# One of three int16 shifts of a softmax group moved from VectorE to GpSimd, with a smaller backlog limit and a wider pace limit

## Chip, cores, metric

One core of one Trainium2 chip. The metric is the device time of one execution in microseconds (us). The kernel before took 1766.27 us (median of 3 runs, 1764.87 to 1768.45).

Engines are named as in the profile: PE (matmuls; PEld is its weight load), ACT (ScalarE), DVE (VectorE), POOL (GpSimd), SP (DMA issue). "Granted clock" is the PE clock that the throttle let through, as a share of full speed.

## The reference, cut to what matters

Two layers, each attention and then a gated feed-forward block (2048 tokens, width 512, 32 heads of 16, feed-forward width 1792):

```
x = x + attention(layernorm(x));  x = x + ffn(layernorm(x))      # twice
scores = q @ k.T * 16 ** -0.5;  p = softmax(scores);  o = p @ v  # 32 heads, 2048 x 2048 each
```

The scores make 4096 tiles of 128 x 512 that need an exponential.

## The kernel before

At build time the program runs a time model of all engines and records one fixed instruction order for each ("the plan"). On the chip every engine follows its order and waits on semaphores. A cost in the model that differs from the chip doesn't make the result wrong; it makes the order a bad one.

Exponentials come in groups of 12 tiles, filled in four slots of three tiles. In an ordinary group ACT does all 12. In a *vector group* ACT does two tiles of each slot and DVE the third: it turns the score into the bits of a float16 (tile `fPI`: scale, bias and conversion to int16 give a straight-line approximation of 2^x). To make the approximation better, DVE adds 256, 512 and 768 to the integers (quarter octaves, tiles `fPP`), and PE multiplies all four versions with suitably scaled copies of V. These three additions are the *shifts*, each 128 x 2048 int16.

```python
    DVE_LATE = 3.0          # backlog limit, us of planned DVE work
    LAG = 6                 # pace limit, pieces of the feed-forward stage
    ...
    def port_at(eng, t):    # the plan's model of the shared port: DVE shift against Pool instruction
        for a, b in reversed(port["dve" if eng == "pool" else "pool"][-12:]):
            if a <= t < b:
                return b
        return t
    ...
    def vector_group():
        if pend.get(("PI", dg_no[0] % NPI)):
            return False
        late = max(0.0, sch.free["dve"] - now[0]) + sum(op[3] for j in jobs["dve"] for op in j[2])
        late += 0.6 * len(shifts)
        return late < DVE_LATE
    ...
            # is the next group a vector group?
            d = size == 3 and (layer or u) and vector_group() and behind() < LAG
    ...
            # a_slot: the third tile of a slot, on DVE; after the fourth one, the three shifts
            def then(o):
                ...
                if r == 3:
                    for ph in range(1, NPH):
                        shift(uk, c, g, m, gi, ph)
            dve(0, [(lambda e: e.tensor_scalar(PI[:, gi, 512 * r:512 * (r + 1)], bank(b0 + n - 1), DBIAS, 0.0,
                                               op0=ALU.add, op1=ALU.max), [bks[-1]], [("PI", gi, r)], 0.6)], then)
    ...
    def shift(uk, c, g, m, gi, ph):
        ...
        shifts.append((s, [(lambda e: e.tensor_scalar(PP[:, s, :], PI[:, gi, :], int(OCT) * ph // NPH, None,
                                                      op0=ALU.add),
                            [("PI", gi, r) for r in range(4)], [("PP", s)],
                            2.8 if ph in POOLED else 0.6)], then, ph in POOLED))      # 2.8, 0.6: planned us
    POOLED = ()
    ...
    def behind():           # "post": output projection and feed-forward of a query block, beside the next attention
        ...
        return PIECES * f - pace["n"]
    def post_tol():
        if pace["haste"] or behind() > LAG:
            return 99.0
        return 1.0 if behind() > 0 else 0.1
```

When PE has nothing to do for long, the plan adds filler matmuls (`fONB`,`fZV`) to keep its clock up.

## Time and profile before

| | us |
|---|---|
| span | 1766.0 |
| ACT busy, of it exponentials | 1602.1, 1527.4 |
| PE busy (ends are modelled) | 1614.0 |
| DVE busy, of it conversions / shifts | 1276.4, 504.3 / 393.7 |
| POOL busy | 208.2 |
| vector groups | 192 of 320 (768 conversions / 4) |

From the page of the kernel before: busy us of each engine, the span in 40 slices (tenths busy; PEclk in tenths of full clock), and the chain that ended last.

```profile
PE 1614.0 (91%) x16180; PEld 497.5 (28%) x16349; DVE 1276.4 (72%) x2103; ACT 1602.1 (91%) x1488; POOL 208.2 (12%) x226
...
DVE  5799996577856878538653799767895588856853
ACT  2699889999999999999899999999999999999932
POOL 2502011011110011010330110201011000101000
PEclk9999999999999999999999999999999999999999
...
ACT 61%; PE 21%; DVE 14%; issue 1%; POOL 1%; DMA 1%; SPq 0%; DVEq 0%; POOLq 0%
```

ACT is nearly full (8 or 9 tenths) from the third slice to the third last and makes most of the chain: exponentials are the limit. DVE is full only in the dense stage of slices 3 to 6 and in slices 24, 25 and 30.

Groups of instructions of the kernel before, shapes kept apart. Columns: line, engine, operation, out<-in, shapes, count, then busy us and mean ns of one, then idle time just before and what ended it.

```profile
L1128 ACT ACTIVATE fPT<-fPS 128x1024 bf16<-128x1024 f32 x992 | 932.4, 1078 | 43.2 <-PE fPS L1123 41.5
L1128 ACT ACTIVATE fPT<-fPS 128x1536 bf16<-128x1536 f32 x448 | 611.4, 1509 | 40.0 <-PE fPS L1123 39.5
L1162 DVE TENSOR_SCALAR fPI<-fPS 128x512 int16<-128x512 f32 x768 | 504.3, 683 | 65.5 <-PE fPS L1123 63.9
L1184 DVE TENSOR_SCALAR fPP<-fPI 128x2048 int16<-128x2048 int16 x576 | 393.7, 716 | 4.4 <-PE fPS L1233 3.4
L1253 PE MATMUL fPS<-fONB,fZV 128*17 128x512 bf16 x3356 | 256.6, 386 | 5.0 <-POOL fONB L344 4.1 <-DVE fOS L808 0.8
L651 POOL TENSOR_SCALAR fVD<-fVP 128x544 f16<-128x544 f16 x24 | 38.4, 1600 | 44.8 <-DVE fVP L659 43.4
L545 POOL TENSOR_SCALAR fHT<-fX,fLNS 128x512 bf16<-128x512 f32 x36 | 27.3, 773 | 0.9
L651 POOL TENSOR_SCALAR fVD<-fVP 128x136 f16<-128x136 f16 x24 | 15.5, 648 | 85.7 <-DVE fVP L659 84.4
```

### The profile page before, as it was taken

To read this page: it belongs to the slowest core of one execution; us is meant where nothing else is said; L and a number is where in the kernel's file an instruction comes from. 1 tells how busy PE (TensorE), PEld (TensorE's weight loads), DVE (VectorE), ACT (ScalarE), POOL (GpSimd) and SP (SyncE) were. 2 spreads that over 40 slices of the span, in tenths; PEclk is the share of its full clock that TensorE was granted. 3 is DMA by queue.
4 is the path that set the end of the run, shared out by engine and by line. 5 is a ranking of instruction groups with operands and counts; after the bars stand their busy time and mean duration, and the time that the engine had idled before them with its cause. 6 is when DMAs were issued, how large, how long until landed. Compare 5 with 4: busy or idle time off the path is not lost.

```text
span 1766.0 us, 38383 instructions
## 1 busy us (share of the span) xinstructions
PE 1614.0 (91%) x16180; PEld 497.5 (28%) x16349; DVE 1276.4 (72%) x2103; ACT 1602.1 (91%) x1488; POOL 208.2 (12%) x226
## 2 busy tenths in 40 slices
PE   7898989999899999989999989999989899999998
PEld 3422222222222222332333322222222222222233
DVE  5799996577856878538653799767895588856853
ACT  2699889999999999999899999999999999999932
POOL 2502011011110011010330110201011000101000
PEclk9999999999999999999999999999999999999999
DMA  5200000143111530125214100013401142012513
GB/s 156 73 2 17 2 15 10 47 119 115 41 37 41 162 86 17 43 57 158 65 48 133 41 18 9 17 49 102 148 18 31 51 134 91 23 39 81 152 27 104
DMA packets 138705, 114.00 MB, mean 65 GB/s; under 512 B 12320, under 2 KB 126240, under 8 KB 138528
## 3 DMA queue, kind: packets, MB, share of 16 engines
q1 hardware_dynamic: 134256, 103.07, 20.3%
q0 software_dynamic: 4272, 8.39, 1.7%
q8 instruction: 133, 2.18, 0.5%
q14 instruction: 44, 0.36, 0.1%
HBM read 97.78 MB, written 6.82 MB: 59 GB/s over the span
## 4 chain that ended last, share of the span: by engine, by line
ACT 61%; PE 21%; DVE 14%; issue 1%; POOL 1%; DMA 1%; SPq 0%; DVEq 0%; POOLq 0%
ACT fPT L1128 58%; DVE fPI L1162 6%; PE fPS L575 6%; PE fPS L1123 5%; DVE fPP L1184 5%; PE fPS L1233 4%; PE fPS L1253 3%; ACT fHT L1094 2%; PE fPS L932 2%; DVE fQ L618 1%; PE fPS L638 1%; DVE fHT L545 1%; ACT L1094 1%; DMA fX<-in_A_x_dram 0%; POOL fVD L651 0%
## 5 line engine op out<-in xcount | busy, mean ns | idle before, releaser
L1128 ACT ACTIVATE fPT<-fPS 128x1024 bf16<-128x1024 f32 (+1 forms) x1440 | 1527.4, 1212 | 83.1 <-PE fPS L1123 81.1
L1123 PE MATMUL fPS<-fQ,fKT 32*128 32x512 bf16 x4096 | 554.2, 385 | 71.5 <-ACT fPT L1128 56.0
L1162 DVE TENSOR_SCALAR fPI<-fPS 128x512 int16<-128x512 f32 x768 | 504.3, 683 | 65.5 <-PE fPS L1123 63.9
L1233 PE MATMUL fPS<-fPT,fVP 128*17 128x512 bf16 x3328 | 432.9, 384 | 13.1 <-ACT fPT L1128 6.7
L1184 DVE TENSOR_SCALAR fPP<-fPI 128x2048 int16<-128x2048 int16 x576 | 393.7, 716 | 4.4 <-PE fPS L1233 3.4
L1123 PEld LDWEIGHTS fPS<-fQ,fKT 32*128 32x128 bf16 x4096 | 138.8, 91 | 617.3 <-ACT fPT L1128 527.1
L1233 PE MATMUL fPS<-fPP,fVD 128*17 128x512 f16 x2304 | 302.3, 381 | 6.4 <-DVE fPP L1184 6.1
L1253 PE MATMUL fPS<-fONB,fZV 128*17 128x512 bf16 x3356 | 256.6, 386 | 5.0 <-POOL fONB L344 4.1
L575 PE MATMUL fPS<-fXNT,fWR 128*128 128x512 bf16 x831 | 212.9, 381 | 20.3 <-DVE fHT L918 8.9
L1233 PE MATMUL fPS<-fPI,fVP 128*17 128x512 f16 x768 | 217.4, 384 | 0.5 <-DVE fPP L1184 0.5
L918 DVE TENSOR_TENSOR fHT<-fPS,fHT 128x512 bf16<-128x512 f32 x112 | 77.0, 689 | 140.0 <-PE fPS L575 92.4
L1233 PEld LDWEIGHTS fPS<-fPT,fVP 128*17 128x17 f16 x3328 | 100.0, 87 | 177.4 <-issue 127.2
L767 POOL TENSOR_TENSOR fAT<-fOS,fRB 128x512 bf16<-128x512 f32 x32 | 42.6, 1330 | 830.1 <-DMA fRB<-rscr 784.8
L895 DVE CAST fHT<-fPS 128x512 bf16<-128x512 f32 x98 | 67.5, 689 | 85.4 <-PE fPS L575 85.3
L932 PE MATMUL fPS<-fWR,fHT 128*128 128x512 bf16 x407 | 115.4, 382 | 6.5 <-issue 4.8
L575 PEld LDWEIGHTS fPS<-fXNT,fWR 128*128 128x128 bf16 x896 | 71.9, 97 | 123.2 <-DVE fHT L918 21.6
L1253 PEld LDWEIGHTS fPS<-fONB,fZV 128*17 128x17 f16 x3356 | 77.0, 91 | 84.5 <-issue 40.7
L1233 PEld LDWEIGHTS fPS<-fPP,fVD 128*17 128x17 f16 x2304 | 69.8, 88 | 88.8 <-issue 48.0
L651 POOL TENSOR_SCALAR fVD<-fVP 128x544 f16<-128x544 f16 (+1 forms) x48 | 53.9, 1124 | 130.5 <-DVE fVP L659 127.8
L808 DVE COPY fOS<-fPS 128x512 f32<-128x512 f32 x64 | 43.8, 684 | 23.8 <-PE fPS L1233 23.7
L533 POOL TENSOR_SCALAR fLNS<-fMV 128x4 f32<-128x4 f32 x16 | 6.3, 395 | 460.3 <-DVE fMV L526 460.2
L1233 PEld LDWEIGHTS fPS<-fPI,fVP 128*17 128x17 f16 x768 | 47.4, 88 | 34.2 <-issue 19.3
(60 smaller groups left out, 693.8 us busy)
## 6 DMA issues: line engine op xcount, KB each, us to landing
fWR<-in_B_w_down_dram SPq DMA_DIRECT2D x189, 256.0 KB, 3.0
fWR<-in_B_w_gate_dram SPq DMA_DIRECT2D x56, 256.0 KB, 3.3
fWR<-in_B_w_up_dram SPq DMA_DIRECT2D x56, 256.0 KB, 2.9
fRB<-rscr SPq DMA_DIRECT2D x256, 32.0 KB, 1.8
fX<-in_A_x_dram POOLq DMA_DIRECT2D x7, 1024.0 KB, 5.4
xscr<-fX SPq DMA_DIRECT2D x16, 256.0 KB, 2.1
fX<-xscr SPq DMA_DIRECT2D x4, 1024.0 KB, 6.2
fAT<-fATS SPq DMA_DIRECT2D x128, 16.0 KB, 1.8
```

Source lines behind the costliest of these rows:

```text
L575: ins = e.matmul(bank(bs[0])[:, 0:cols], lhsT=l, rhs=r_, start=(i == 0), stop=(i == n - 1))
L651: job("pool", 2, [(lambda e, dst=dst, src=src, ph=ph: e.tensor_scalar(dst, src, 2.0 ** (-ph / NPH), None, op0=ALU.mult), [("VP", c, k) for ...
L895: evac_job(1, b, [(lambda e: e.tensor_copy(HT[:, ft, :], bank(b)), [BK[b]], [("HT", ft)], 0.6)], got(("gate", layer, qb, ft)))
L918: (lambda e: e.tensor_tensor(HT[:, ft, :], bank(b), HT[:, ft, :], op=ALU.mult), [BK[b], ("HT", ft)], [("HT", ft)], 0.62)], got(("up", laye ...
L932: ins = e.matmul(bank(b)[:, 0:D], lhsT=HT[:, ft, i * 128:(i + 1) * 128], rhs=WR[:, s, jj * D:(jj + 1) * D], start=(ft == 0), stop=(ft == N ...
L1094: sch.op("act", lambda e, lo=lo, hi=hi: e.activation(HT[:, lo:hi, :], HT[:, lo:hi, :], ACTF.Gelu_apprx_tanh), r=keys, w=keys, cost=0.05 + ...
L1123: ins = e.matmul(bank(b0 + k), lhsT=KT[32 * j:32 * j + 32, c, kt * 128:(kt + 1) * 128], rhs=Q[32 * j:32 * j + 32, qs, :], start=True, stop ...
L1128: o = sch.op("act", lambda e: e.activation(PT[:, p, 0:512 * na].rearrange("p (a b) -> p a b", a=na), PS[:, b0:b0 + na, :], ACTF.Exp, scale ...
L1162: dve(0, [(lambda e: e.tensor_scalar(PI[:, gi, 512 * r:512 * (r + 1)], bank(b0 + n - 1), DBIAS, 0.0, op0=ALU.add, op1=ALU.max), [bks[-1]], ...
L1184: shifts.append((s, [(lambda e: e.tensor_scalar(PP[:, s, :], PI[:, gi, :], int(OCT) * ph // NPH, None, op0=ALU.add), [("PI", gi, r) for r ...
L1233: ins = e.matmul(PS[32 * j:32 * j + VW, ACC, :], lhsT=l, rhs=r_, start=a, stop=z, tile_position=(0, 32 * j), skip_group_check=True)
L1253: ins = e.matmul(PS[32 * j:32 * j + VW, ACC, :], lhsT=ZV[:, :], rhs=ones, start=False, stop=False, tile_position=(0, 32 * j), skip_group_c ...
```

## The change

Intent: let Pool, which is 12% busy, take one of the three shifts in groups 0 to 3 of each five, so that DVE can serve more vector groups; admit vector groups only at a smaller DVE backlog; and let the feed-forward pieces fall further behind before vector groups stop.

```diff
-    DVE_LATE = 3.0
+    DVE_LATE = 2.0
...
-    LAG = 6
+    LAG = 24
...
+        pooled = ph == 1 and m < NM - 1
...
-                            [("PI", gi, r) for r in range(4)], [("PP", s)], 2.8 if ph in POOLED else 0.6)], then, ph in POOLED))
+                            [("PI", gi, r) for r in range(4)], [("PP", s)], 2.8 if pooled else 0.6)], then, pooled))
...
-    POOLED = ()
```

## The prediction

> **What bounds the kernel now.** The page's busy table: ScalarE (ACT) 1602 of 1766 us, PE 1614 (ends modelled), VectorE (DVE) 1276, Pool 208. The chain of waits is 61% ACT, nearly all softmax exponentials. Stretches of 44 us show ACT busy 42 us or more in most between 88 and 1678 us; it idles mostly in head and tail. Exponentials leave ACT in "vector groups": of 12 score tiles DVE takes 4. The groups table has 768 DVE conversions: 192 of 320 groups. A vector group turns four 3-tile exponentials (1509 ns, start to start about 1.36 us) into four 2-tile ones (1078 ns, 0.92 us): ACT saves 1.7 us. DVE pays 4 x 0.68 + 3 x 0.68 us, about 4.7; PE pays 3 more quads of matmuls of about 0.22 us.
>
> Where groups are missing: the DVE timeline shows none for about 25 us at the start of each feed-forward ("post") stage (497 to 522 us, 538 to 556 us), because the pieces are more than 6 behind their pace. In dense attention (88 to 221 us) DVE is 93% busy or more.
>
> **What the change does.** (1) One of three shifts of groups 0 to 3 of five goes to Pool: DVE pays 0.68 us less per such group. Estimate for a Pool shift: the Pool normalisation takes 772 ns for 512 columns and small Pool ops about 250 to 330, so about 0.9 ns a column: 2.1 to 2.4 us for 2048. The shift is DVE's four-per-cycle form (2048 elements in 0.6 to 0.68 us); the Trainium skill, "SBUF — State Buffer", section "Who interferes with whom", says that such a DVE instruction and a Pool instruction take a shared port pair exclusively, the second fully blocked. The trace agrees in kind: this shift reaches 1765 ns, the Pool multiply 2298 (median 1271). Per group the port is taken about 2.2 + 1.3 us of 3.7 to 4.2: it fits, tightly. (2) The pace limit 24 admits vector groups in the post's opening and takes urgency from the pieces. (3) The backlog limit 2.0 admits fewer, offsetting part.
>
> **Sum.** Vector groups rise from 192 to about 222: 30 x 1.7 = 51 us less ACT work. PE must do the same pieces in less time, plus 30 x 0.65 = 20 us. Its filler matmuls, 839 quads or about 180 us, leave room on average, almost none in the slices of the down projection (8 to 24 fillers). I take 75%: 38 us. Predicted 1728 us, 1697 to 1757 eight times in ten. Faster by over 2%: 0.52; within 2%: 0.43; slower by over 2%: 0.05.
>
> **What would show it.** Conversions 768 to about 890; exponential busy 1527 to about 1475 us; about 175 shifts on Pool at 2.1 to 2.8 us, Pool busy about 630 us; DVE busy within 5% of 1276; mean DVE shift up from 716 to 800 ns or more by port waits; filler matmuls 3356 down to about 2700; conversions in the openings of the posts; head and tail unchanged within 5 us.
>
> **What would make it wrong.** Port waits longer than the schedule assumed would stall DVE, then ACT through score banks: the gain shrinks or goes. If PE is the limit in post stages, ACT idles there before score matmuls, or posts slip into the layer change or the tail. If the smaller backlog limit rejects as many groups as the rest admits, conversions and time stay. If posts never block vector groups and the port holds, conversions could pass 950 and the time fall below 1697.

## The result

The changed kernel took 2347.45 us (median of 4 runs, 2337.86 to 2438.24), the kernel before 1767.36 us. The ratio is 1.3264 (95% interval 1.3211 to 1.3317). Ratios here and below are the mean time of one kernel's fast runs over the mean of the other's fast runs of the same rounds, so not quite the ratio of the medians. Three of the four runs are fast runs, 2337.86 to 2350.98 us at a granted clock of 0.854 to 0.862, mean 2344.3 us. The profiled run is slow (2438.24 us, clock 0.691), so I take counts and waits from its trace and compare times with fast runs only.

The page of the changed kernel, the same lines:

```profile
PE 2018.8 (83%) x16097; PEld 529.5 (22%) x16097; DVE 1819.6 (75%) x2143; ACT 1618.5 (66%) x1488; POOL 1214.5 (50%) x403
...
DVE  5778888876886877777843878887888778878752
ACT  2676767667766676666678776665776677666641
POOL 2776663454753447535540456535675345544520
PEclk7766666666666676666677766666767667666677
...
PE 49%; DVE 26%; POOL 17%; issue 4%; ACT 2%; DMA 1%; SPq 0%; POOLq 0%; DVEq 0%
```

ACT is no longer full anywhere and has all but left the chain (61% to 2%). DVE and POOL now make 43% of it. The groups of the changed kernel:

```profile
L1128 ACT ACTIVATE fPT<-fPS 128x1024 bf16<-128x1024 f32 x1116 | 1091.3, 1026 | 442.0 <-PE fPS L1123 437.7
L1185 POOL TENSOR_SCALAR fPP<-fPI 128x2048 int16<-128x2048 int16 x177 | 990.6, 5606 | 821.9 <-DVE fPI L1162 781.0 <-PE fPS L1232 35.5 <-DVE fPP L1185 2.6
L1185 DVE TENSOR_SCALAR fPP<-fPI 128x2048 int16<-128x2048 int16 x492 | 813.3, 1690 | 26.2 <-PE fPS L1232 24.9
L1162 DVE TENSOR_SCALAR fPI<-fPS 128x512 int16<-128x512 f32 x892 | 597.2, 685 | 225.7 <-PE fPS L1123 221.0
L1128 ACT ACTIVATE fPT<-fPS 128x1536 bf16<-128x1536 f32 x324 | 458.2, 1451 | 277.1 <-PE fPS L1123 274.9
L1252 PE MATMUL fPS<-fONB,fZV 128*17 128x512 bf16 x2732 | 270.4, 482 | 5.0 <-POOL fONB L344 4.2 <-DVE fOS L808 0.8
```

The counts are those that the prediction named: 892 conversions (about 890), 177 Pool shifts (about 175), 2732 fillers (about 2700). The durations are not. A Pool shift takes 5606 ns; the plan had 2800. A DVE shift takes 1690 ns in the mean. The minimum, median and maximum of each in the changed kernel:

```profile
L1185 DVE TENSOR_SCALAR fPP<-fPI x492: 621/693/5859, 93.5 to 2345.7; 128x2048 int16<-128x2048 int16 x164
L1185 POOL TENSOR_SCALAR fPP<-fPI x177: 5358/5611/6937, 93.5 to 2328.5; 128x2048 int16<-128x2048 int16 x177
```

The DVE shift's median is what it was (683 before, 693 now). Its mean rises because some take as long as a whole Pool shift (5859). The Trainium skill, "SBUF — State Buffer", section "Who interferes with whom", says that a DVE instruction in a mode that uses two ports and a Pool instruction take one shared port pair exclusively, for the whole instruction, so that the second one blocks. I take the shift, 2048 columns in 0.68 us, to be in such a mode. The trace looks like that, but two other things happen at once: PE also waits for the late Pool results, and the PE clock is down. The longest waits of PE's matmuls in the changed kernel (us, times, longest); in the kernel before, they waited 10.6 us for shifts:

```profile
PE fPS L1232 <- DVE fPP L1185: 171.0, 69, 4.9
PE fPS L1232 <- POOL fPP L1185: 143.3, 99, 3.1
```

The experiments take these apart as far as they can.

### The profile page after: what moved, and what is told of

It is laid out like the page before. It is cut to its first block, busy times and chain, and to the rows that moved or that the text cites. A ratio compares the mean times of both kernels' runs of the same rounds, so it can differ in the third digit from the quotient of the medians.

```text
span 2436.4 us, 38363 instructions
## 1 busy us (share of the span) xinstructions
PE 2018.8 (83%) x16097; PEld 529.5 (22%) x16097; DVE 1819.6 (75%) x2143; ACT 1618.5 (66%) x1488; POOL 1214.5 (50%) x403
## 4 chain that ended last, share of the span: by engine, by line
PE 49%; DVE 26%; POOL 17%; issue 4%; ACT 2%; DMA 1%; SPq 0%; POOLq 0%; DVEq 0%
DVE fPP L1185 16%; POOL fPP L1185 15%; PE fPS L1232 14%; PE fPS L575 13%; PE fPS L1123 11%; DVE fPI L1162 5%; PE fPS L1252 5%; PE fPS L932 4%; ACT fPT L1128 2%; PE fPS L638 1%; DVE fQ L618 1%; PE fPS L552 1%; DVE fHT L895 1%; POOL fVD L651 1%; DVE fOKL L734 1%
## 5 line engine op out<-in xcount | busy, mean ns | idle before, releaser
L1185 POOL TENSOR_SCALAR fPP<-fPI 128x2048 int16<-128x2048 int16 x177 | 990.6, 5606 | 821.9 <-DVE fPI L1162 781.0
L1185 DVE TENSOR_SCALAR fPP<-fPI 128x2048 int16<-128x2048 int16 x492 | 813.3, 1690 | 26.2 <-PE fPS L1232 24.9
L1162 DVE TENSOR_SCALAR fPI<-fPS 128x512 int16<-128x512 f32 x892 | 597.2, 685 | 225.7 <-PE fPS L1123 221.0
L1123 PE MATMUL fPS<-fQ,fKT 32*128 32x512 bf16 x4096 | 633.3, 448 | 42.6 <-DVE fPI L1162 19.4
L1232 PE MATMUL fPS<-fPT,fVP 128*17 128x512 bf16 x3204 | 519.3, 454 | 116.3 <-DVE fPP L1185 71.3
L1232 PE MATMUL fPS<-fPP,fVD 128*17 128x512 f16 x2676 | 394.4, 486 | 162.8 <-POOL fPP L1185 96.5
L1232 PE MATMUL fPS<-fPI,fVP 128*17 128x512 f16 x892 | 293.4, 455 | 39.8 <-DVE fPP L1185 34.5
L575 PE MATMUL fPS<-fXNT,fWR 128*128 128x512 bf16 x896 | 300.4, 480 | 27.4 <-DVE fHT L895 19.1
L932 PE MATMUL fPS<-fWR,fHT 128*128 128x512 bf16 x448 | 158.0, 474 | 0.1
L767 POOL TENSOR_TENSOR fATS<-fOS,fRB 128x512 bf16<-128x512 f32 x32 | 49.3, 1540 | 29.4 <-DMA fRB<-rscr 29.4
```

The lines of the kernel that those rows point to most:

```text
L575: ins = e.matmul(bank(bs[0])[:, 0:cols], lhsT=l, rhs=r_, start=(i == 0), stop=(i == n - 1))
L767: job("pool", 1, [(lambda e: e.tensor_tensor(dst, OS[:, os_, :], RB[:, slot, :], op=ALU.mult), [("OS", os_)] + [("RB", slot, j) for j in r ...
L932: ins = e.matmul(bank(b)[:, 0:D], lhsT=HT[:, ft, i * 128:(i + 1) * 128], rhs=WR[:, s, jj * D:(jj + 1) * D], start=(ft == 0), stop=(ft == N ...
L1123: ins = e.matmul(bank(b0 + k), lhsT=KT[32 * j:32 * j + 32, c, kt * 128:(kt + 1) * 128], rhs=Q[32 * j:32 * j + 32, qs, :], start=True, stop ...
L1232: ins = e.matmul(PS[32 * j:32 * j + VW, ACC, :], lhsT=l, rhs=r_, start=a, stop=z, tile_position=(0, 32 * j), skip_group_check=True)
```

## Experiments

Theory: the Pool shift is twice as long as planned, and what costs time is DVE standing behind it at the port. Rivals: PE waiting for late Pool results; the two limits; the PE clock falling by itself; a plan that is merely wrong about a cost.

### e1_no_pool: the limits without the Pool shift

```diff
-        pooled = ph == 1 and m < NM - 1
+        pooled = False
```

> The changed kernel with all three shifts on DVE again; pace limit 24 and backlog limit 2.0 stay. Theory (the Pool shift alone is to blame): 1715 to 1745 us, mean clock at or above 0.98, DVE shifts back to a mean of 700 to 730 ns, conversions 850 or more. Rival (the new limits crowd PE, or the PE clock falls by itself with more vector groups): 1800 us or more with a clock under 0.95.

Measured: 1729.53 us (1728.79 to 1733.58), ratio to before 0.9789 (0.9772 to 0.9805), clock 0.997, 880 conversions. Page line and DVE shifts of this kernel:

```profile
PE 1591.2 (92%) x15951; PEld 492.4 (29%) x16125; DVE 1392.4 (81%) x2299; ACT 1557.6 (90%) x1488; POOL 209.4 (12%) x226
...
L1185 DVE TENSOR_SCALAR fPP<-fPI 128x2048 int16<-128x2048 int16 x660 | 447.2, 716 | 6.0 <-PE fPS L1232 4.2
```

So the limits alone make the kernel 2.1% faster (the interval lies across the 2% mark, but far from 1), and 220 vector groups do not pull the clock down. The whole loss, about 615 us (2344.3 - 1729.5; the kernel before ran at 1767.4 and 1767.9 us beside them), belongs to the Pool shift.

### e2_pool_only: the Pool shift without the limits

```diff
-    DVE_LATE = 2.0
+    DVE_LATE = 3.0
...
-    LAG = 24
+    LAG = 6
```

> The kernel before with only the Pool shift (pace limit 6, backlog limit 3.0). Theory (Pool alone): 2150 us or more, Pool shifts 5.4 to 5.7 us each, DVE shifts with a mean above 1500 ns. Rival (the limits, or their combination with Pool): under 1900 us.

Measured: 2258.63 us, ratio 1.2779 (1.2758 to 1.2801), clock 0.881 to 0.887; 160 Pool shifts with a mean of 5574 ns; 428 DVE shifts with a mean of 1535 ns. It also failed the correctness check by a hair (relative error 0.020005); this version is only a probe of time. The Pool shift does it without the limits.

### e4_probe: the Pool shift by itself

Seven forms of Pool instruction, three of each back to back, appended at the end of the kernel before, where DVE runs no shifts. Five of the forms:

```python
e.tensor_scalar(PP[:, 0, :], PI[:, 0, :], 256, None, op0=ALU.add)                    # the shift: 2048 int16
e.tensor_scalar(PP[:, 0, 0:1024], PI[:, 0, 0:1024], 256, None, op0=ALU.add)          # half of it
e.tensor_scalar(PP[:, 0, 0:1024].bitcast(F32), OS[:, 0, :], 1.0, None, op0=ALU.add)  # 512 float32
e.tensor_scalar(PP[:, 0, 0:512].bitcast(BF), OS[:, 0, :], 1.0, None, op0=ALU.add)    # 512 float32 to bf16
e.tensor_tensor(PP[:, 0, :].bitcast(I32), PI[:, 0, :].bitcast(I32), <int32 constant>, op=ALU.add)   # 1024 int32
```

> The kernel before with seven forms of Pool instruction, three of each, appended in the tail, where DVE runs no shifts. It measures the Pool shift by itself. If Pool is slow by itself (theory): the 2048-element int16 form takes 5.2 to 5.6 us, the 1024-element form about half. If the 5.6 us of the changed kernel are made of waiting for DVE (rival): 2.1 to 2.8 us here. Forms on 32-bit words (1024 int32 elements, two inputs) about 2.5 us. The time of the kernel itself stays within 5 us of the tail's slack plus these ops, about 1810 us.

Measured (one look): 1787.89 us, most of the additions fit the tail. The timeline of Pool in this kernel; columns are start us, us of all three, instruction, count:

```profile
1722.92 16.39 POOL L1420 TENSOR_SCALAR fPP<-fPI 128x2048 int16<-128x2048 int16 x3
1739.40 8.52 POOL L1422 TENSOR_SCALAR fPP<-fPI 128x1024 int16<-128x1024 int16 x3
1748.00 4.63 POOL L1424 TENSOR_SCALAR fPP<-fOS 128x512 f32<-128x512 f32 x3
1752.71 4.64 POOL L1426 TENSOR_SCALAR fPP<-fOS 128x512 bf16<-128x512 f32 x3
...
1762.15 5.83 POOL L1430 TENSOR_TENSOR fPP<-fPI,fCI 128x1024 int32<-128x1024 int32 x3
```

The shift takes 5.46 us (16.39 / 3), though DVE runs no shifts here. DVE is not quite absent: four of its normalisations come up during the first Pool instructions, and the first three take 5.6 us each and end 0.28 us after the Pool shift that they stand behind. So they wait for Pool, not Pool for them; and in e10_probe2 a one-operation shift with no DVE instruction beside it takes 5.44 us (from 1746.29). The Pool shift is slow by itself, not slowed by DVE. From 512 to 2048 columns the time grows by (5.46 - 1.54) / 1536 = 2.55 ns a column, whatever the data type. And the float32 to bf16 form takes 1.55 us for 512 columns, where the normalisation, with the same shapes and types, takes 0.77. Something other than type and size is at work (see the second probe). I timed by blocks of three because the Trainium skill, "Perfetto Trace Analysis", section "GPSIMD Engine Instruction", advises start-to-start spacing for Pool; here single durations (5358 ns at least) agree with it.

### e5_shadow: Pool instructions that nobody waits for

The plan of e1_no_pool, with PE, ACT and DVE unchanged to the instruction, plus one Pool instruction of the same length per group whose output nobody reads.

```diff
+        if ph == 1 and m < NM - 1:
+            was = sch.free["pool"]
+            sch.op("pool", lambda e: e.tensor_scalar(SHD[:, 0:1984], <1984 int16 of WO>, 1, None, op0=ALU.add),
+                   r=[("PI", gi, 3), ("WO",)], w=[("SHD",)], cost=0.0)
+            sch.last_r[("PI", gi, 3)].pop("pool")     # it does not really read PI: nobody waits for it
+            sch.free["pool"] = was                    # and the plan does not see it
```

> The schedule of e1_no_pool instruction for instruction on PE, ACT and DVE, plus a Pool instruction of the same length per group (1984 int16 inputs, reading a weight tile, its output read by nobody), released by the group's last conversion. Nobody waits for its result, so only the shared port can hurt. Theory A (port lock makes DVE's shifts wait): 2000 us or more, DVE shifts with a mean above 1500 ns and maxima near 5.6 us, clock under 0.95. Rival B (PE waits for the late Pool result; the port matters little): within 2% of e1_no_pool.

Measured: 2560.90 us, ratio 1.4482 (1.4458 to 1.4506), clock 0.81. An instruction that produces nothing costs 831 us. One case from the timelines of DVE and Pool in this kernel:

```profile
157.17 1.28 DVE L1163 TENSOR_SCALAR fPI<-fPS 128x512 int16<-128x512 f32 x2
158.37 4.50 DVE L1193 TENSOR_SCALAR fPP<-fPI 128x2048 int16<-128x2048 int16 x1
```

```profile
156.61 5.71 POOL L1188 TENSOR_SCALAR fSHD<-fWO 128x1984 uint8<-128x1984 int16 x1 [6.98 <-DVE fPI L1163]
```

The Pool instruction runs from 156.61 to 162.32. The conversions at 157.17 read PSUM and run through at full speed. The shift that begins at 158.37 takes 4.50 us and ends 0.55 us after Pool. That is the usual case: of the 171 DVE shifts that start while a shadow runs, 168 end only after it. All that time DVE, which works in order, cannot do the next conversion, and a score bank (the PSUM buffer of a score tile) stays occupied. PE feels the late shifts even more directly:

```profile
PE fPS L1240 <- DVE fPP L1193: 508.9, 180, 5.6
```

PE's matmuls with V waited 508.9 us for DVE shifts (13.2 in e1_no_pool), its score matmuls 28.1 us for conversions (5.3), and ACT waited 861.2 us for scores (85.3). So waiting for the results of Pool shifts is not needed for a loss of this size; the port is enough. One rival remains: a shadow also holds up Pool's own useful work behind it. The trace makes it small: the direct waits of other engines for Pool's results come to 32 us in all here and 16 us in e1_no_pool. The trace of this run agrees with the cited section.

### e6_shadow_half and e14_shadow_short: shorter shadows

e6_shadow_half cuts the shadow to 992 columns. e14_shadow_short has all 1984 columns in a faster form (`1, 1.0, op0=ALU.add, op1=ALU.mult`), which the second probe below suggested.

> e5_shadow with the unread Pool instruction cut to 992 columns: about 2.7 us in place of 5.4, the length that the plan of the changed kernel had assumed. e1_no_pool took 1729.5 us, e5_shadow 2560.9. Theory (time that DVE's shifts stand behind Pool instructions, growing faster than their length): 1820 to 2000 us, DVE shifts with a mean of 900 to 1200 ns. Rival (a fixed cost per Pool instruction, whatever its length): over 2300 us.

> The plan of e1_no_pool for PE, ACT and DVE, plus an unread Pool instruction of about 1.9 us per group (two-operation form). If the remaining 56 us of e7_int32 over e1_no_pool are port waits: 1760 to 1800 us, mean DVE shift 780 to 860 ns. If they come from the plan with pooled shifts or from waits for Pool's results: within 1% of e1_no_pool, 1725 to 1747 us.

Measured: e6_shadow_half 1820.25 us (ratio 1.0299), e14_shadow_short 1882.09 us (ratio 1.0655). DVE shifts and shadow of e6_shadow_half, then of e14_shadow_short:

```profile
L1193 DVE TENSOR_SCALAR fPP<-fPI 128x2048 int16<-128x2048 int16 x660 | 546.5, 865 | 4.1 <-PE fPS L1240 2.6
L1188 POOL TENSOR_SCALAR fSHD<-fWO 128x992 uint8<-128x992 int16 x169 | 519.6, 3074 | 738.6 <-DVE fPI L1163 738.5
```

```profile
L1193 DVE TENSOR_SCALAR fPP<-fPI 128x2048 int16<-128x2048 int16 x660 | 594.9, 938 | 3.7 <-PE fPS L1240 2.1
...
L1188 POOL TENSOR_SCALAR fSHD<-fWO 128x1984 uint8<-128x1984 int16 x169 | 349.5, 2068 | 942.4 <-DVE fPI L1163 942.1
```

The four kernels with one and the same plan for PE, ACT and DVE line up by how long DVE's shifts wait, not by how long the Pool instruction is:

| kernel | Pool instruction, mean us | DVE shifts, busy us | more than e1_no_pool | span of the same run | more than e1_no_pool |
|---|---|---|---|---|---|
| e1_no_pool | none | 447.2 | | 1727.4 | |
| e6_shadow_half | 3.07 | 546.5 | 99.3 | 1813.6 | 86.2 |
| e14_shadow_short | 2.07 | 594.9 | 147.7 | 1879.0 | 151.6 |
| e5_shadow | 5.43 | 1119.0 | 671.8 | 2559.6 | 832.2 |

In the first two rows of shadows, a microsecond of port wait costs about a microsecond of time. My expectation for e14_shadow_short was too low (1760 to 1800), because I took the loss to grow with the length. A 2.07 us instruction did more harm than a 3.07 us one. It is not met more often: 141 DVE shifts start while a shadow runs in e14_shadow_short, 300 in e6_shadow_half. But in e14_shadow_short 139 of the 141 end only after the shadow, as in e5_shadow; in e6_shadow_half 192 of the 300 end while it still runs, 99 of them at full speed. One case from the timelines of Pool and DVE in e6_shadow_half:

```profile
128.83 3.30 POOL L1188 TENSOR_SCALAR fSHD<-fWO 128x992 uint8<-128x992 int16 x1 [5.53 <-DVE fPI L1163]
130.59 0.68 DVE L1193 TENSOR_SCALAR fPP<-fPI 128x2048 int16<-128x2048 int16 x1
```

The 992-column shadow, then, does not block DVE for its whole length, against the cited section (the 1024-column form in e4_probe doesn't either: a DVE normalisation that begins 0.11 us into it takes 1.25 us and ends 1.45 us before it), and e6_shadow_half is not simply a half of e5_shadow. So the duration alone does not tell how long a Pool instruction keeps DVE out; why this form leaves a gap the runs do not show. In e5_shadow the loss is larger than the port wait by 160 us. The granted clock is 0.81 there against 0.997; the Trainium skill, "TensorE: Matmul & The Clock Gate", section "What's actually happening", says that PE's clock is set by how busy PE has recently been, which would make the low clock a consequence of PE's waits. The profiled runs fit (clock 0.988 in e6_shadow_half, 0.975 in e14_shadow_short, 0.81 in e5_shadow, in the order of their waits), but none separates the clock's share of the 160 us.

### e7_int32 and e8_int32_true: the same shift, short

The shift as an exact add of 1024 32-bit words, 1.94 us in the probe (5.83 / 3). The halves stay below 0x7c00, so nothing carries over. The Trainium skill, "GPSIMD Engine Reference", section "Engine selection", says that a two-input Pool add on 32-bit integers is exact. The outputs are right.

```diff
-        e.tensor_scalar(PP[:, s, :], PI[:, gi, :], int(OCT) * ph // NPH, None, op0=ALU.add)
+        e.tensor_tensor(PP[:, s, :].bitcast(I32), PI[:, gi, :].bitcast(I32), <0x01000100>, op=ALU.add)   # if pooled
```

e8_int32_true also tells the plan 2.0 us in place of 2.8.

> The changed kernel with one thing replaced: the Pool shift is done as an exact add of 1024 32-bit words (0x01000100 to each, so both 16-bit halves move by 256; they stay below 0x7c00, so nothing carries), which the probe timed at 1.94 us against 5.46 us. Same plan, same dependencies, same use of the shared port. Theory (the length of the Pool instruction, 5.5 us where the plan had 2.8, is the whole fault): 1710 to 1745 us, correct, clock 0.98 or more, DVE shifts with a mean of 750 to 1000 ns. Rival (any Pool shift against this many DVE shifts breaks the order): above 1850 us.

> As e7_int32, with the plan told 2.0 us for the Pool shift in place of 2.8. If what matters is that the plan is near the truth: 1705 to 1745 us, within 1.5% of e7_int32 either way.

Measured: e7_int32 1785.60 us (ratio 1.0103), clock 0.987 to 0.993, Pool shifts 2132 ns, DVE shifts 890 ns in the mean; e8_int32_true 1785.04 us (ratio 1.0091). Nothing but the Pool instruction was replaced in e7_int32, and 559 of the 615 us are gone (2344.3 - 1785.6). But it missed the range I gave (1710 to 1745): 56 us over e1_no_pool remain, although DVE has 168 shifts fewer to do. Telling the plan the true cost gave nothing.

### e3_true_cost: the slow shift, known to the plan

```diff
-  2.8 if pooled
+  5.6 if pooled
```

> The changed kernel with the slow Pool shift, but the plan told 5.6 us in place of 2.8. If the loss comes from the plan being wrong (engines ordered for a port that should be free): 1780 to 1900 us, clock 0.95 or more. If the port itself is overloaded by a 5.5 us instruction per group whatever the order: 2100 us or more.

Measured: 2126.08 us, ratio 1.2023, clock 0.918 to 0.921 (also a hair over the error limit, 0.0200025). An honest plan makes it 218 us faster than the changed kernel (2344.3 to 2126.1), with 151 Pool shifts and 736 conversions, and it is still 358 us slower than the kernel before. So the wrong cost may be part of the loss, though this plan also admits fewer vector groups (184 against 223); and the one order that the planner found with the true cost does not carry a 5.5 us Pool instruction in most groups.

### e9_probe2 and e10_probe2: why the normalisation was no guide

e9_probe2 did not build (one of its forms, a 16-bit two-input add on Pool, does not compile) and was not run.

> The kernel before with six forms of Pool instruction, three of each, in the tail. It asks why the Pool normalisation (772 ns for 512 columns, the number that the prediction scaled) was no guide. If the form decides (two operations with scalars read from memory against one with an immediate): the 2048-column int16 form with two pointer scalars takes 2.0 to 2.6 us and that with an immediate 5.4 us. If it is the data type: both take about 5.4 us and only the float32 to bf16 form is short.

e10_probe2 is the same without that form: the shift with an immediate; with one scalar from memory; with two scalars from memory (add, then multiply by 1.0); with two immediates (add 256, multiply by 1.0); the 512-column float32 to bf16 form with two scalars; the int32 add.

> As written for e9_probe2, without the 16-bit two-input form that did not compile. If the form decides: the 2048-column int16 form with two pointer scalars takes 2.0 to 2.6 us, that with an immediate 5.4 us. If it is the data type: both about 5.4 us and only the float32 to bf16 form with pointer scalars is near 0.8 us for 512 columns.

Measured, in this order; Pool's timeline in e10_probe2, without the int32 add (5.83 us for three, as in e4_probe):

```profile
1718.66 16.39 POOL L1423 TENSOR_SCALAR fPP<-fPI 128x2048 int16<-128x2048 int16 x3
1735.15 16.59 POOL L1425 TENSOR_SCALAR fPP<-fPI,fCF 128x2048 int16<-128x2048 int16 x3
1751.84 6.35 POOL L1427 TENSOR_SCALAR fPP<-fPI,fCF 128x2048 int16<-128x2048 int16 x3
1758.27 5.87 POOL L1429 TENSOR_SCALAR fPP<-fPI 128x2048 int16<-128x2048 int16 x3
1764.24 2.52 POOL L1431 TENSOR_SCALAR fPP<-fOS,fCF 128x512 bf16<-128x512 f32 x3
```

With one operation the shift takes 5.46 or 5.53 us; with two operations 2.12 or 1.96 us. Neither the type nor where the scalar comes from matters much. On Pool, this `tensor_scalar` with a second operation is 2.8 times *faster* than with one (5.46 / 1.96). The normalisation has two operations and is on the fast side; the shift and the V scaling (1600 ns for 544 columns) have one and are on the slow side.

### e13_two_op: that one argument, in the changed kernel

```diff
-        e.tensor_scalar(PP[:, s, :], PI[:, gi, :], int(OCT) * ph // NPH, None, op0=ALU.add)
+        e.tensor_scalar(PP[:, s, :], PI[:, gi, :], int(OCT) * ph // NPH, 1.0, op0=ALU.add, op1=ALU.mult)   # if pooled
```

> The changed kernel with one argument pair changed: the Pool shift adds 256 and then multiplies by 1.0, a two-operation form of the same instruction, which the second probe timed at 1.96 us against 5.46 us. Theory (the length of the Pool instruction): as e7_int32, 1770 to 1800 us, clock 0.98 or more, Pool shifts 1.9 to 2.4 us. Rival (something else about the 32-bit form helped in e7_int32): above 1900 us.

Measured: 1785.37 us (1784.73 to 1785.68), ratio 1.0105 (1.0088 to 1.0122), clock 0.990 to 0.993, correct. Shifts of this kernel:

```profile
L1187 DVE TENSOR_SCALAR fPP<-fPI 128x2048 int16<-128x2048 int16 x492 | 421.7, 895 | 13.4 <-PE fPS L1234 11.9
L1185 POOL TENSOR_SCALAR fPP<-fPI 128x2048 int16<-128x2048 int16 x177 | 378.0, 2136 | 818.5 <-DVE fPI L1162 762.3 <-PE fPS L1234 35.5 <-DVE fPP L1187 20.3
```

As e7_int32, by another instruction: the length of the Pool instruction is the cause of most of the loss, not its form. How much of that loss is DVE waiting at the port, and how much is PE waiting for late Pool shifts (143.3 us of direct waits in the changed kernel), no run separates: a shorter instruction ends both.

What is left, 56 us over e1_no_pool, fits the port: e14_shadow_short shows that 2 us Pool instructions alone cost that plan 152 us, and the DVE shifts take 890 ns in the mean in e7_int32 against 716 in e1_no_pool. PE's waits for Pool shifts, by contrast, are down to 0.4 us in e13_two_op, so late Pool results are not what is left. The plans differ, so this is not a subtraction, and I call it likely, not shown.

### e11_lag_only and e12_late_only: where the 2.1% come from

The kernel before with one limit each: `LAG = 24`, or `DVE_LATE = 2.0`.

> The kernel before with only the pace limit at 24. If the gain of e1_no_pool (2.1%) comes from the pace limit: 1725 to 1745 us with 880 conversions or more. If the two limits only work together: 1755 to 1775 us.

> The kernel before with only the backlog limit at 2.0. If the smaller backlog is what helps: 1730 to 1750 us. If it merely rejects vector groups: 1760 to 1785 us with fewer than 768 conversions.

Measured: 1758.97 us (ratio 0.9948, 868 conversions) and 1761.93 us (ratio 0.9964, 740 conversions); together, e1_no_pool, 0.9789 with 880. Alone they give 0.5% and 0.4%, together 2.1%: most of the gain needs both. The pace limit alone takes about as many exponentials off ACT as both do, yet saves little; in its trace the single wait of ACT in the tail grows from 30.1 us before to 40.4 us, against 31.3 in e1_no_pool. That is 9 of the 33 us between the two profiled runs. Most of the rest is ACT waiting for scores before exponentials (103.4 against 85.3 us) and slightly more exponential work (1489.2 against 1482.9 us).

## Why the prediction was wrong

The forecast was 1728 us; the kernel took 2347.

- **Right: what bounds the kernel, and what the change admits.** ACT was the limit. Conversions 892 (forecast about 890), Pool shifts 177 (about 175), fillers 2732 (about 2700). With the Pool shift taken out again, the time is 1729.5 us and exponentials are busy 1482.9 us (forecast 1475). That agreement is partly luck: the forecast counted on the Pool shift's help for those groups, and e1_no_pool has them without it.
- **The step that failed: "about 0.9 ns a column: 2.1 to 2.4 us for 2048".** It measured 5.46 us alone and 5.61 in the kernel. I scaled the wrong instruction. The trace before held a Pool instruction of the same form as the shift (`tensor_scalar`, one operation, an immediate): the V scaling, 648 ns for 136 columns and 1600 ns for 544. Its slope, 952 / 408 = 2.33 ns a column, gives 648 + 1912 x 2.33 = 5.1 us. I took the normalisation because its shape looked more alike, and did not ask why the two disagreed.
- **What followed from it: "it fits, tightly".** With the true length, one group needs 5.5 us of Pool and 2 x 0.66 us of DVE shifts at the port, 6.8 us, where a group has 3.7 to 4.2. The forecast's list named "port waits longer than the schedule assumed", but as a reason for the gain to shrink or go, not for a loss of a third. It also named a path, "would stall DVE, then ACT through score banks". The traces show mainly another: PE, which follows its order, waits for the late shifts themselves (171.0 us for DVE's and 143.3 for Pool's in the changed kernel, against 19.4 for conversions in score banks), score matmuls come late behind that, and ACT starves (its idle before exponentials goes from 83 to 719 us). These waits are from the slow profiled run; the fast run of e5_shadow shows the same path. The lower granted clock (0.86 in the fast runs against 0.997) may add to it; its share was not separated.
- **Also missing: that port waits cost about their full length (or more, in e5_shadow).** I expected a mean DVE shift of 800 ns or more and no harm from it. In e14_shadow_short 938 ns meant 152 us. Even a Pool shift of the forecast length makes the kernel slower than with none (1785 against 1729.5 us).
- **Wrong on DVE and POOL busy.** Forecast within 5% of 1276 and about 630 us; measured 1819.6 and 1214.5 in the slow profiled run, and DVE 1392.4 in e1_no_pool.

The Trainium skill, "Perfetto Trace Analysis", section "Optimizing Scalar/DVE Operations", warns that moving work between DVE and Pool might not help, because a two-port DVE instruction holds the shared port. These runs agree: the best of all tried versions is the one that moves nothing, e1_no_pool, 2.1% faster than the kernel before.

## What to carry to other kernels

Before moving work to an engine, measure the very instruction there: same operation count, same operands; if two durations in the trace disagree about the price, find out why before using either. When two engines share a lock and one of them works in order on the critical path, count the lock time of both per unit of work, and expect each wait to cost its full length. Look in the trace whether the lock is really held as long as the instruction lasts. When a change bundles several edits, build each alone: here the two limits were worth 2.1% and the third edit cost 615 us.

## What the Trainium skill lacked or had wrong

- "GPSIMD Engine Reference", section "Engine selection", calls one-input Pool instructions roughly line-rate. The one-operation `tensor_scalar` measured 2.55 ns a column, about three cycles at the page's 1.2 GHz; only the two-operation form comes near a cycle a column (1.96 us for 2048 columns). No page says that a second operation makes it 2.8 times faster (5.46 against 1.96 us).
- "SBUF — State Buffer", section "Who interferes with whom", holds in most runs: DVE shifts of 0.68 us took up to 5.86 us beside 5.6 us Pool instructions, and conversions from PSUM kept 0.68 us. But it says that the pair is taken for the whole instruction, and in e6_shadow_half 192 of the 300 DVE shifts that started during a 992-column Pool instruction ended before it did, 99 of them at full speed. What it doesn't say is the price: port waits of 99 and 148 us cost 86 and 152 us of kernel time, and the shorter Pool instruction (2.07 us) cost more than the longer (3.07 us).
- "Perfetto Trace Analysis", section "GPSIMD Engine Instruction", calls Pool durations unreliable. Here single durations and blocks of three agreed (5.36 us at least against 5.46 us).
